# Norm of the second segment among the last output projection, first pair's split weights kept for the second, other PSUM banks

## The chip, the cores and the metric

The kernel runs on one core of a Trainium2 chip. The metric is the device time of one execution in microseconds; the kernel before took 904.81 us, the median of three runs (904.62 to 905.78). The engines are TensorE (PE, with its weight loads as PEld), VectorE (DVE), ScalarE (ACT), GpSimd (POOL) and SyncE (SP), which issues all transfers here. [...]

## The reference

A layer norm with modulation, an attention in four segments with a memory carried from one to the next, and a gated feed-forward part, for 2048 rows of 512 columns, all in fp32. The change lies in the second half. Cut to that:

```python
mod = (_silu(c) @ w_mod).reshape(c.shape[0], 6, 1, -1)
sa, ca, ga, sb, cb, gb = (mod[:, i] for i in range(6))
h = _layernorm(x) * (1 + ca) + sa
x = x + ga * _A_ref(h, A_wq, A_wk, A_wv, A_wo, A_beta)   # attention, its last step is o @ wo
h = _layernorm(x) * (1 + cb) + sb
g = h @ w_gate                       # 512 x 1376
u = h @ w_up                         # 512 x 1376
x = x + gb * ((g * u) @ w_down)      # 1376 x 512
```

## The kernel before, in words

**Precision.** TensorE multiplies in fp32r. An operand is therefore split into a rounded part and the rest, by an ACT copy (hi) and a subtraction on DVE or POOL (lo), and a product is three matmuls: hi x hi, hi x lo, lo x hi (`six`: two such products, six matmuls, for two chunks of the contraction).

**Stages.** Up to about 505 us the attention runs; its steps, the four output projections and the first norm of the feed-forward stage are woven by hand. `wo_op`, `wo_row` and `wo_add` are the output projection of a segment, which ends in x1 = x + projection, written to DRAM (`x1d`). `lnC(s)` (L523) then loads segment s of x1 in four tiles of 128 rows, takes mean and variance on DVE, the root by Ln and Exp on ACT, normalises on DVE (L557), transposes on TensorE (`ctp`, L88), and evicts with the modulation on ACT (`chf`, L566).

**The feed-forward stage** works on pairs of segments: pair 0 is segments 0 and 1, pair 1 is 2 and 3. The 1376 columns of gate and up are eleven tiles of 128, the last (tile 10, `LAST`) of 96. Two neighbouring tiles by the two segments of a pair are one 2 x 2 block product, done with seven products instead of eight. That needs sums of the weights and of the activations:
- `prepare` calls `wprep(n)` (L432) for a unit n, which is gate or up of two tiles: it loads the raw weights `cr`, forms four sums `cs` on POOL (L448 to L452), rounds raw and sums to `cwH` on ACT (L456) and subtracts to `cwL` on POOL (L457). `cwH` and `cwL` are 128 x 1792 fp32, 0.92 MB each, in three slots, slot -n mod 3. For tile 10 `xprep` does the same without sums. `wdprep` (L1244) loads a tile of w_down, multiplies by gb and splits it on DVE and ACT. In pair 0 the down weights of tiles 0, 1 and 10 (`dHp`, `dLp`) lie in the space of weight slot 1.
- `build(p)` (L1171) forms the activations' sums `t` on POOL (L1186) and splits them, `bH` on ACT (L1178), `bL` on DVE (L1179).
- `unit(n)` (L1313) runs the seven products into the banks Z (`sm`), Y (`tb`) and X (`ms0`, `ms1` in turn). ACT copies p1, p5 and y out, DVE adds (c0, c1, c2, L1304), and for up the product g*u (L1299) is formed on POOL or DVE and split into `mH` (ACT, L1240) and `mL` (DVE, L1241). The last two products of a unit (`seven`, `four`, kept in `tail`) are issued in the next unit.
- `direct` (L1361) does tiles 0, 1 and 10 of pair 0 and tile 10 of pair 1 without sums: Xg, Xu of the first segment, with a copy q between the halves, then Yg, Yu of the second. `dirbank` gives its banks in turn from `DB`; before, starting with ms0.
- `down` (L1262) multiplies by the down weights into a bank `acc`, and DVE adds it to `xa` (L1274), which holds x1 and goes to `out` at the end of the pair.

Pair 0 thus starts with lnC(1) and direct tiles 0, 1 and 10 mixed, then down of tiles 0, 1 and 10 for segment 0, then the direct tiles' second segment (the Ys), then units 2, 4, 6, 8. `down` items wait in a list and fill between the products. lnC(2) and lnC(3) run among pair 0's units, build(1) in its last unit.

**What sets the order.** `pe` and `pin` chain TensorE's instructions and the pinned loads by hand in program order. Other instructions are placed by the scheduler, and each engine runs its own in that order. SP issues the transfers in one queue, in order, and with eight completion lanes: each waits for the transfer eight before it. Buffers with a tag and `bufs` are reused in turn, and the next writer waits for the last reader.

## Time and profile before

| | |
|---|---|
| median of three runs | 904.81 us |
| profiled execution | 904.86 us |
| its span (first to last instruction) | 903.1 us |
| TensorE busy, mean granted clock | 856.8 us, 0.990 |
| POOL, DVE, ACT busy | 501.2, 655.1, 475.5 us |
| moved by DMA | 105.70 MB, mean 117 GB/s |
| feed-forward stage, first Xg to last acc | 522.0 to 899.5 us |

A line of the profile gives start, duration, engine, line of the kernel, operation, output <- input, shape, and in brackets the idle time before it and what ended that. In views of stretches the numbers behind the length are busy times of PE, PEld, DVE, ACT and POOL, then TensorE's granted clock, the DMA engines' share and GB/s. Tile names are those of the kernel without buffer numbers. A matmul's duration is longer than the distance to the next, since they overlap; the distance is the pace.

### The profile page before, as it was taken

What the parts mean: (1) busy time and instruction counts of PE and PEld (TensorE: products, weight loads), DVE (VectorE), ACT (ScalarE), POOL (GpSimd) and SP (SyncE); (2) the same over time, 40 slices, a digit from 0 to 9 for tenths busy, and PEclk for the clock granted to TensorE, in tenths of its full rate; (3) what the DMA queues carried; (4) which work ended last, traced back from release to release, by engine and by line L of the source; (5) the groups of instructions that cost most, each with busy time, mean ns of one, the idle gap of its engine ahead of it and who ended that gap; (6) DMA issues with size and microseconds to landing.
All of it is one profiled execution on the core that took longest, in us unless ns stands there. A gap on an engine that the chain in (4) does not pass through costs nothing.

```text
span 903.1 us, 14396 instructions
## 1 busy us (share of the span) xinstructions
PE 856.8 (95%) x4975; PEld 600.8 (67%) x4976; DVE 655.1 (73%) x1711; ACT 475.5 (53%) x725; POOL 501.2 (56%) x607
## 2 busy tenths in 40 slices
PE   8989999989999999999999987989999799999998
PEld 5755656556665566665666665768888577788876
DVE  7598777888788877878886275875956976646544
ACT  3747757687676865767445443433444433343320
POOL 4445536565564763856235326876844977757310
PEclk8999999999999999999999999999999999999999
DMA  7555444554554545466664381213211064211002
GB/s 222 158 159 133 121 111 129 151 158 125 133 133 133 152 145 133 115 185 185 187 209 135 101 282 47 57 37 94 69 50 47 1 197 129 70 47 36 12 1 93
DMA packets 78617, 105.70 MB, mean 117 GB/s; under 512 B 11792, under 2 KB 49680, under 8 KB 78544
## 3 DMA queue, kind: packets, MB, share of 16 engines
q1 hardware_dynamic: 78400, 104.76, 39.4%
q8 instruction: 39, 0.64, 0.3%
q14 instruction: 34, 0.28, 0.1%
q10 hardware_dynamic: 144, 0.02, 0.0%
HBM read 76.43 MB, written 28.05 MB: 116 GB/s over the span
## 4 chain that ended last, share of the span: by engine, by line
PE 71%; DVE 11%; ACT 6%; POOL 6%; DMA 3%; issue 2%; SPq 0%; DVEq 0%; POOLq 0%; ACTq 0%
PE acc L1271 12%; PE tb L85 8%; PE q L85 6%; PE k L85 6%; PE Xg L1216 5%; PE Xu L1216 5%; DVE q L39 5%; PE wops L85 5%; PE vps L85 4%; PE kps L85 4%; PE Yg L1216 3%; PE Yu L1216 3%; PE qps L85 2%; POOL cwL L457 2%; ACT pt L331 2%
## 5 line engine op out<-in xcount | busy, mean ns | idle before, releaser
L39 DVE CUSTOM_DVE_ANT_0 q<-q,cmask 128x384 f32<-128x384 f32 (+3 forms) x512 | 246.6, 508 | 49.9 <-PE q L85 39.8
L331 ACT ACTIVATE pt<-k 128x1024 f32<-128x1024 f32 x160 | 163.8, 1024 | 64.5 <-PE k L85 63.4
L337 POOL TENSOR_SCALAR_AFFINE_SELECT pt<-pt 128x256 f32<-128x256 f32 (+1 forms) x224 | 96.8, 446 | 166.0 <-ACT pt L331 163.7
L85 PE MATMUL q<-kst,qst 96*128 96x384 bf16 (+3 forms) x512 | 101.6, 299 | 11.6 <-DVE nm L39 9.7
L85 PE MATMUL k<-qst,kst 98*128 98x384 bf16 (+3 forms) x512 | 97.1, 302 | 5.0 <-ACT pt L331 4.9
L1274 DVE TENSOR_TENSOR xa<-xa,acc 128x512 f32<-128x512 f32 x95 | 64.7, 682 | 48.0 <-PE acc L1271 46.6
L85 PE MATMUL tb<-pt,v 128*32 128x512 f32 (+3 forms) x1024 | 75.5, 436 | 0.0
L39 DVE DVE_READ_ACCUMULATOR2_ANT nm<- 128x1 f32 x512 | 72.2, 141 | 0.0
L85 PEld LDWEIGHTS <-kst 98*128 98x128 bf16 x512 | 37.7, 98 | 49.5 <-issue 43.3
L85 PEld LDWEIGHTS <-qst 96*128 96x128 bf16 x512 | 43.1, 97 | 38.1 <-issue 14.3
L1271 PE MATMUL acc<-dH,mH 128*128 128x512 f32 (+1 forms) x150 | 59.7, 398 | 2.1 <-ACT mH L1240 2.1
L1271 PE MATMUL acc<-dH,mL 128*128 128x512 f32 (+1 forms) x150 | 59.5, 397 | 0.4 <-DVE mL L1241 0.4
L1271 PE MATMUL acc<-dL,mH 128*128 128x512 f32 (+1 forms) x150 | 59.3, 396 | 0.0
L85 PEld LDWEIGHTS tb<-pt,v 128*32 128x32 f32 x1024 | 28.6, 109 | 38.6 <-issue 33.8
L457 POOL TENSOR_TENSOR cwL<-cr,cwH 128x512 fp32r<-128x512 f32 (+1 forms) x36 | 40.1, 1131 | 21.5 <-ACT cwH L456 21.4
L457 POOL TENSOR_TENSOR cwL<-cs,cwH 128x1024 fp32r<-128x1024 f32 x18 | 48.3, 2684 | 1.2 <-ACT cwH L456 1.2
L1299 POOL TENSOR_TENSOR c0g<-c0g,c0u 128x512 f32<-128x512 f32 x9 | 11.7, 1296 | 56.4 <-DVE c0u L1304 37.7
L363 ACT ACTIVATE tsb<-tb 128x512 f32<-128x512 f32 x32 | 19.0, 595 | 41.0 <-PE tb L85 41.0
L1271 PEld LDWEIGHTS acc<-dH,mH 128*128 128x128 f32 (+1 forms) x150 | 28.2, 188 | 9.9 <-ACT mH L1240 2.5
L1271 PEld LDWEIGHTS acc<-dH,mL 128*128 128x128 f32 (+1 forms) x150 | 28.3, 189 | 7.3 <-DVE mL L1241 0.9
L1271 PEld LDWEIGHTS acc<-dL,mH 128*128 128x128 f32 (+1 forms) x150 | 28.3, 188 | 6.7
L1216 PE MATMUL Xu<-bH,cwH 128*128 128x512 f32 (+1 forms) x68 | 28.1, 413 | 3.5 <-DVE c2u L1304 2.7
(374 smaller groups left out, 2240.3 us busy)
## 6 DMA issues: line engine op xcount, KB each, us to landing
wm<-in_w_mod_dram SPq DMA_DIRECT2D x24, 256.0 KB, 4.0
kd<-k SPq DMA_DIRECT2D x16, 384.0 KB, 2.5
kst<-kd SPq DMA_DIRECT2D x32, 192.0 KB, 3.2
qd<-q SPq DMA_DIRECT2D x16, 384.0 KB, 2.9
qst<-qd SPq DMA_DIRECT2D x32, 192.0 KB, 3.7
crd<-in_w_down_dram SPq DMA_DIRECT2D x20, 256.0 KB, 2.8
cr<-in_w_gate_dram SPq DMA_DIRECT2D x9, 512.0 KB, 3.9
cr<-in_w_up_dram SPq DMA_DIRECT2D x9, 512.0 KB, 4.4
```

What stands on the lines that cost most here:

```text
L39: i = getattr(self.eng, name)(*a, **k)
L85: return pe(nc.tensor.matmul(*a, **k))
L331: ex = act.activation(pt, kp, AF.Exp, scale=0.25)
L337: sels[u, i] = nc.gpsimd.affine_select(w, w, pattern=[[0, w.shape[1]], [1, P]], compare_op=ALU.is_ge, fill=0.0, base=0, channel_multiplier=-1)
L363: act.activation(tsbs[u], tbs.pop(u), AF.Copy)
L457: gp.tensor_sub(wl[:, d], v, wh[:, d].bitcast(F32))
L1216: pe(nc.tensor.matmul(ps[0:n], a, b[:, k], start=first and c == 0, stop=last and c == 5, skip_group_check=True))
L1271: pe(nc.tensor.matmul(ps, a[0:m, t * P:(t + 1) * P], b[0:m], start=j == 0, stop=j == n - 1))
L1274: vec.tensor_add(xa, xa, ps)
L1299: (vec if psum else nc.gpsimd).tensor_mul(g[0:n], g[0:n], v[0:n])
```

## The change

- **lnC(1) earlier.** It is made at slot 2 of the last step, right after the first three groups of `wo_op(3)`: its four loads are issued there, a tile's statistics follow each `wo_row`, Ln and Exp come ahead of the last group of `wo_op(3)`, and the normalisation follows the four `wo_add`. x1_1 lies in the projection's weight pool (`wpool`, tag "orl"), which now stays open to the end. All transposes of segment 1 run between direct tiles 0 and 1, and build(0) starts before direct tile 1.
- **Weights kept.** In pair 0 each unit's cwH and cwL, tile 10's and the down weights' splits are stored to DRAM (`keep`), 59 SP transfers more in all. In pair 1 they are loaded (`fetch`) and each tile is rounded in place by ACT copies of 1024 and 768 columns. POOL's sums and subtractions and DVE's work on w_down disappear there, but for unit 0, which pair 0 never split. Pair 1's units go in the order 2, 4, 6, 8, 0.
- **Other banks.** `ndir` starts at 2, so direct starts with tb and sm, and pair 0's last Ys lie in ms0 and ms1.
- **Less memory.** Temporaries 13 to 8, `add` writes in place, one buffer for cs, one tile for the sums t, so each sum waits until the splits of the one before have been made; the order of the sums is 5, 3, 6, 4, 7. Tile 10 and w_down's last tile are padded with zeros to 128.

```diff
@@ -392,30 +392,56 @@
     LAST = NF - 1
     units = [(0, nm, i) for i in range(2, LAST, 2) for nm in "gu"]
     CH = len(units)
-    units += [(1, "x", LAST)] + [(1, nm, i) for i in range(0, LAST, 2) for nm in "gu"]
+    units += [(1, "x", LAST)] + [(1, nm, i) for i in (2, 4, 6, 8, 0) for nm in "gu"]
     NU = len(units)
+    ENDS = (8, 0)
     wslot, plain = {}, {}
+    wkeep, dkeep = {}, {}
+
+    def keep(key, tiles, store):
+        n = tiles[0].shape[1]
+        store[key] = [dram.tile([P, n], F32, name=f"kept{x}{key[0]}{key[1]}") for x in "HL"]
+        for dst, t in zip(store[key], tiles):
+            nc.sync.dma_start(dst, t.bitcast(F32))
+
+    def fetch(key, tiles, store):
+        for a, d in zip(tiles, store[key]):
+            pin(nc.sync.dma_start(a.bitcast(F32), d))
+        yield
+        n = tiles[0].shape[1]
+        for a in tiles:
+            for i in range(0, n, 1024):
+                b = a[:, i:min(n, i + 1024)]
+                act.activation(b, b.bitcast(F32), AF.Copy)
+                yield
 
     def xprep(n, tag, pool, rpool):
 
-        raw = rpool.tile([P, KT, 2, P], F32, tag="raw0", name=f"cr{n}", bufs=1)
         wh = pool.tile([P, 7, 2, P], F32R, tag=f"wh{tag}", name=f"cwH{n}", bufs=1)
         wl = pool.tile([P, 7, 2, P], F32R, tag=f"wl{tag}", name=f"cwL{n}", bufs=1)
         m = ft[LAST][1]
+        for j, nm in enumerate("gu"):
+            plain[int(n == CH), LAST, nm] = wh[:, 0:4, j], wl[:, 0:4, j]
+        flat = [a.rearrange("p a b c -> p (a b c)")[:, 0:8 * P] for a in (wh, wl)]
+        if n == CH:
+            yield from fetch(("x", LAST), flat, wkeep)
+            return
+        raw = rpool.tile([P, KT, 2, P], F32, tag="raw0", name=f"cr{n}", bufs=1)
+        nc.gpsimd.memset(raw[:, :, :, m:], 0.0)
         for j, w in enumerate((w_gate, w_up)):
             pin(nc.sync.dma_start(raw[:, :, j, 0:m], w.rearrange("(k p) f -> p k f", p=P)[:, :, LAST * P:]))
         yield
-        act.activation(wh[:, 0:4, :, 0:m], raw[:, :, :, 0:m], AF.Copy)
-        nc.gpsimd.tensor_sub(wl[:, 0:4, :, 0:m], raw[:, :, :, 0:m], wh[:, 0:4, :, 0:m].bitcast(F32))
-        for j, nm in enumerate("gu"):
-            plain[int(n == CH), LAST, nm] = wh[:, 0:4, j], wl[:, 0:4, j]
+        act.activation(wh[:, 0:4], raw, AF.Copy)
+        nc.gpsimd.tensor_sub(wl[:, 0:4], raw, wh[:, 0:4].bitcast(F32))
+        yield
+        keep(("x", LAST), flat, wkeep)
         yield
 
...
         for w, nm in ((w_gate, "g"), (w_up, "u")):
-            raws[nm] = raw = rpool.tile([P, KT, P], F32, tag="cr", name=f"cr{nm}{i}", bufs=4)
+            raws[nm] = raw = wpool.tile([P, D], F32, tag="wor", name=f"cr{nm}{i}", bufs=2).rearrange("p (k c) -> p k c", c=P)
             pin(nc.sync.dma_start(raw, w.rearrange("(k p) f -> p k f", p=P)[:, :, i * P:(i + 1) * P]))
         yield 0.0
         gp = nc.gpsimd
@@ -432,15 +458,19 @@
     def wprep(n, tag, pool, rpool):
 
         _, nm, i = units[n]
-        raw = rpool.tile([P, KT, 2, P], F32, tag=f"raw{(n + 1) % 2}", name=f"cr{n}", bufs=1)
+        if (nm, i) not in wkeep:
+            raw = rpool.tile([P, KT, 2, P], F32, tag=f"raw{(n + 1) % 2}", name=f"cr{n}", bufs=1)
         wh = pool.tile([P, 7, 2, P], F32R, tag=f"wh{tag}", name=f"cwH{n}", bufs=1)
         wl = pool.tile([P, 7, 2, P], F32R, tag=f"wl{tag}", name=f"cwL{n}", bufs=1)
         wslot[n] = wh, wl
+        if (nm, i) in wkeep:
+            yield from fetch((nm, i), [a.rearrange("p a b c -> p (a b c)") for a in (wh, wl)], wkeep)
+            return
         views = [w.rearrange("(k p) f -> p k f", p=P)[:, :, i * P:] for w in (w_gate, w_up)]
         gp = nc.gpsimd
         pin(nc.sync.dma_start(raw.rearrange("p k r c -> p k (r c)"), views["gu".index(nm)][:, :, 0:2 * P]))
         yield
-        S = rpool.tile([P, 4, 2, P], F32, tag=f"ws{(n + 1) % 2}", name=f"cs{n}", bufs=1)
...
@@ -1126,6 +1156,8 @@
                 btag[:] = ["ms", "sm", "ms"]
                 us3 = []
                 run(wo_op(3, o3, us3, range(NG - 1), True))
+                lg1 = lnC(1, wpool, lambda: pc, wpool, "orl", 4, lambda name: dbank(name))
+                next(lg1)
             if prev and slot == 4:
                 if (v - 1) % 2 == 0 and v > 8:
                     until((v - 1) // 8, (v - 1) // 2 % 4, 0)
@@ -1150,20 +1182,23 @@
     ps3 = [bank(f"wops3_{t}", shape=(P, 512)) for t in range(4)]
     for t in range(4):
         run(wo_row(ps3[t], t, us3, range(NG - 1)))
+        next(lg1)
     btag[:] = ["sm"]
+    next(lg1)
     run(wo_op(3, o3, us3, (NG - 1,), True))
     for t in range(4):
         run(wo_row(ps3[t], t, us3, (NG - 1,)))
         wo_add(3, t, xr3[t], ps3[t])
+    for t in range(4):
+        next(lg1)
...
-    close(wppool)
...
-    NT, NM = 13, 12
+    NT, NM = 8, 12
...
             pieces[p, j] = hi, lo
 
-        def comb(nm, a, b):
-            r = []
+        T = pc.tile([P, 2, L], F32, tag="ws1", name=f"t{p}", bufs=1)
+
+        def comb(a, b):
             for k in range(2):
-                t = tmp(f"{nm}{p}_{k}")
-                nc.gpsimd.tensor_sub(t, a[k], b[k])
-                r.append(t)
-            return r
-
+                nc.gpsimd.tensor_sub(T[:, k], a[k], b[k])
+            return t
+
+        t = [T[:, k] for k in range(2)]
         b11, b12, b21, b22 = ([hfs[2 * p + c, r][:, k] for k in range(2)] for r in range(2) for c in range(2))
         if p > 0:
             emit(1, b11)
             yield
             emit(2, b21)
             yield
-        t1 = comb("t1", b12, b11)
-        emit(5, t1)
+        emit(5, comb(b12, b11))
         yield
         emit(3, b22)
         yield
-        t2 = comb("t2", b22, t1)
-        emit(6, t2)
-        yield
-        emit(7, comb("t3", b22, b12))
-        yield
-        emit(4, comb("t4", b21, t2))
+        emit(6, comb(b22, t))
+        yield
+        emit(4, comb(b21, t))
+        yield
+        emit(7, comb(b22, b12))
...
@@ -1243,14 +1276,21 @@
 
     def wdprep(p, f, tiles=None):
         f0, n = ft[f]
-        r = tmp(f"crd{p}_{f}")
-        hi, lo = tiles or (bc.tile([P, D], F32R, tag="wd", name=f"d{x}{p}_{f}", bufs=8) for x in "HL")
+        hi, lo = tiles or [bc.tile([P, D], F32R, tag="wd", name=f"d{x}{p}_{f}", bufs=8) for x in "HL"]
+        wds[p, f] = hi, lo
+        if p > 0:
+            yield from fetch(("d", f), (hi, lo), dkeep)
+            return
+        r = tmp(f"crd{p}_{f}") if tiles else wpool.tile([P, D], F32, tag="wor", name=f"crd{p}_{f}", bufs=2)
         pin(nc.sync.dma_start(r[0:n], w_down[f0:f0 + n, :]))
-        yield
-        vec.tensor_mul(r[0:n], r[0:n], gbb[0:n])
-        act.activation(hi[0:n], r[0:n], AF.Copy)
-        vec.tensor_sub(lo[0:n], r[0:n], hi[0:n].bitcast(F32))
-        wds[p, f] = hi, lo
+        if n < P:
+            nc.gpsimd.memset(r[n:], 0.0)
+        yield
+        vec.tensor_mul(r, r, gbb)
+        act.activation(hi, r, AF.Copy)
+        vec.tensor_sub(lo, r, hi.bitcast(F32))
+        yield
+        keep(("d", f), (hi, lo), dkeep)
         yield
 
...
         vec.tensor_add(xa, xa, ps)
-        if fs[0] == LAST - 2:
+        if fs[0] == ENDS[p]:
...
 
-    def add(name, a, b, n=P):
-        r = tmp(name)
-        vec.tensor_add(r[0:n], a[0:n], b[0:n])
-        return r
+    def add(a, b, n=P):
+        vec.tensor_add(b[0:n], a[0:n], b[0:n])
+        return b
 
...
-        finish(p, nm, i, 0, add(f"c0{u}", Z, out_of(f"p1{u}", X)), False)
+        finish(p, nm, i, 0, add(Z, out_of(f"p1{u}", X)), False)
         yield 3
...
         mm(X, 6, False, True)
-        finish(p, nm, i, 1, add(f"c1{u}", X, yy), False)
+        finish(p, nm, i, 1, add(X, yy), False)
...
 
...
     qt = {}
     DB = ["ms0", "ms1", "tb", "sm"]
-    ndir = [0]
+    ndir = [2]
...
     def x_unit(n):
 
-        ndir[0] += 2
         for st in direct(1, LAST, 0):
             yield st
             if st == 1:
@@ -1422,52 +1460,49 @@
             yield from wdprep(p, i + 1)
 
     half = [(c, t) for c in (1, 0) for t in range(4)]
-    lg = lnC(1, pc, pc, pc, "t", NT, dbank)
-    next(lg)
     xp = xprep(-1, 2, pc, pc)
     next(xp)
     dh = pc.tile([P, 7, 2, P], F32R, tag="wh1", name="dHp", bufs=1).rearrange("p a b c -> p (a b c)")
     dl = pc.tile([P, 7, 2, P], F32R, tag="wl1", name="dLp", bufs=1).rearrange("p a b c -> p (a b c)")
     wdp = [wdprep(0, f, (dh[:, j * D:(j + 1) * D], dl[:, j * D:(j + 1) * D])) for j, f in enumerate((0, 1, LAST))]
-    for w in wdp:
+    for w in wdp[:2]:
         next(w)
+    pr0 = prepare(0)
+    next(pr0)
+    next(wdp[2])
     for c, t in half:
         xtile(0, c, t)
     for t in range(4):
         xload2(0, 0, t)
-    pr0 = prepare(0)
-    next(pr0)
     qa = {}
     for f, tag in ((0, "bh7"), (1, "bl7"), (LAST, "bh4")):
         a = pc.tile([P, 2, L], F32, tag=tag, name=f"q0_{f}", bufs=1)
         qa[f] = [a[:, 0], a[:, 1]]
-    for _ in direct(0, 0, 0, qa[0]):
-        next(lg)
+    run(direct(0, 0, 0, qa[0]))
     next(xp)
-    for _ in direct(0, 1, 0, qa[1]):
-        next(lg)
-    next(lg)
+    run(lg1)
+    nb = build(0)
+    next(nb)
+    run(direct(0, 1, 0, qa[1]))
     for w in wdp[:2]:
         next(w)
+    next(nb)
     next(pr0)
-    for _ in direct(0, LAST, 0, qa[LAST]):
-        pass
+    run(direct(0, LAST, 0, qa[LAST]))
     next(wdp[2])
-    next(pr0)
-    nb = build(0)
     for t in range(4):
-        next(lg)
+        next(pr0, None)
         down(0, (0, 1), 0, t)
-    run(lg)
     for t in range(4):
         xload2(0, 1, t)
-    for t in range(4):
-        down(0, (LAST,), 0, t)
-        if t % 2 == 0:
-            next(nb)
     run(pr0)
     pr1 = prepare(1)
     next(pr1)
+    for t in range(4):
+        down(0, (LAST,), 0, t)
+    run(xp)
+    for w in wdp:
+        run(w)
     for f in (LAST, 0, 1):
         for _ in direct(0, f, 1):
             if f != LAST:
...
         for s in (2, 3):
-            yield from lnC(s, pc, (bc, pc)[s % 2], pc, "t", NT, dbank)
+            yield from lnC(s, wpool, lambda: (bc, pc)[s % 2], wpool, "orl", 4, dbank)
...
         pr = prepare(n + 2)
+        if p == 0:
+            keep((nm, i), [a.rearrange("p a b c -> p (a b c)") for a in wslot[n]], wkeep)
         if n == CH - 1:
             nb = build(1)
         for st in (unit if nm != "x" else x_unit)(n):
...
+    close(wppool)
     close(B["bcpool"])
...
```

More of the change, by code (lines that the diff above doesn't have):

```diff
@@ L442, in wprep @@
         yield
-        S = rpool.tile([P, 4, 2, P], F32, tag=f"ws{(n + 1) % 2}", name=f"cs{n}", bufs=1)
+        S = rpool.tile([P, 4, 2, P], F32, tag="ws0", name=f"cs{n}", bufs=1)
         def A(r, c):
@@ L561, in lnC @@
             if d % 2 == 0:
-                hfs[s, d // 2] = hpool.tile([P, 2, L], F32, tag=f"hf{s % 2}{d // 2}", name=f"chf{s}_{d // 2}", bufs=1)
+                hfs[s, d // 2] = hpool().tile([P, 2, L], F32, tag=f"hf{s % 2}{d // 2}", name=f"chf{s}_{d // 2}", bufs=1)
             ps = bk(f"ctp{s}_{d}")
@@ L568, in lnC @@
                 if d % 2 == 0:
-                    pieces[0, 1 + d // 2] = tuple(hpool.tile([P, 2, L], F32R, tag=f"b{x}{1 + d // 2}", name=f"b{x}0_{1 + d // 2}", bufs=1)
+                    pieces[0, 1 + d // 2] = tuple(hpool().tile([P, 2, L], F32R, tag=f"b{x}{1 + d // 2}", name=f"b{x}0_{1 + d // 2}", bufs=1)
                                                   for x in "hl")
@@ L1013, in fill_b @@
         small = lambda name: bank(name, small=True)
-        lg = lnC(0, pb, bc, pb, "x1", 4, small)
+        lg = lnC(0, pb, lambda: bc, pb, "x1", 4, small)
         pr = prep(0, bc, pb)
@@ L1350, in seven @@
             mm(X, 7, False, True)
-            finish(p, nm, i + 1, 1, add(f"c2{u}", X, p5), False)
+            finish(p, nm, i + 1, 1, add(X, p5), False)
         def four():
@@ L1385, in direct @@
             mm(Y, nm, 1, 3, False, True)
-            finish(p, nm, f, 1, add(f"c1{nm}{p}_{f}", Y, q, n), False)
+            finish(p, nm, f, 1, add(Y, q, n), False)
             yield 4
```

## The prediction

> **What bounds the kernel now.** I read the page first, then the busy time of each engine in stretches of 20 us over the feed-forward stage, then TensorE's waits there, then the chain of waits, and last the timeline at the places that the change touches.
>
> ```profile
> span 903.1 us, 14396 instructions
> PE 856.8 (95%) x4975; PEld 600.8 (67%) x4976; DVE 655.1 (73%) x1711; ACT 475.5 (53%) x725; POOL 501.2 (56%) x607
> ```
>
> TensorE is busy 95% of the span, so a gain can only come from its idle time. The changed lines act from about 505 us on. In the next view the columns are the stretch, its length, the busy time of each engine, TensorE's granted clock, and the DMA share and GB/s.
>
> ```profile
> 520.00:540.00 20.00, 18.06 (x77) 13.43 (x76) 15.10 (x28) 9.37 (x19) 4.08 (x4) 1.00 0.96 317
> 540.00:560.00 20.00, 14.89 (x61) 10.57 (x60) 14.06 (x18) 7.28 (x11) 16.80 (x13) 0.91 0.15 54
> 600.00:620.00 20.00, 17.25 (x68) 13.11 (x67) 14.56 (x18) 8.98 (x18) 19.36 (x19) 0.91 0.20 63
> 700.00:720.00 20.00, 15.22 (x58) 10.48 (x57) 18.03 (x18) 9.48 (x17) 20.00 (x14) 0.93 0.00 0
> 720.00:740.00 20.00, 20.00 (x86) 15.41 (x85) 17.42 (x19) 6.66 (x11) 16.06 (x13) 0.99 0.54 172
> ```
>
> TensorE is short of 20 us in a few places only. At 520 to 540 the DMA engines are full. At 700 to 720 POOL is busy for all of it. Its waits between 520 and 900 (what waited, for whom: us in total, times, longest):
>
> ```profile
> PE acc L1271 <- DVE xa L1274: 3.7, 3, 3.0
> PE Xu L1216 <- DVE c2u L1304: 2.7, 2, 2.3
> PE Zg L1216 <- POOL cwL L457: 2.3, 1, 2.3
> PE Zg L1216 <- DVE c1u L1304: 2.1, 1, 2.1
> PE acc L1271 <- ACT mH L1240: 2.1, 1, 2.1
> PE ctp L88 <- DVE x L557: 1.3, 2, 0.8
> PE Xg L1216 <- DVE c1g L1304: 1.3, 1, 1.3
> PE Xg L1216 <- ACT q L1374: 0.9, 1, 0.9
> ...
> PE Xg L1216 <- POOL cwL-1_6784 L409: 0.8, 1, 0.8
> ...
> PE acc L1271 <- DVE mL L1241: 0.4, 1, 0.4
> PE Xu L1216 <- ACT q L1374: 0.3, 1, 0.3
> ```
>
> The chain of waits gives the places (start, us, what):
>
> ```profile
> 522.00 1.41 PE Xg L1216 x6
> ...
> 525.55 5.63 DMA cr-1_6782<-in_w_up_dram
> ...
> 559.50 2.79 PE Yg L1216 x12
> ...
> 578.39 1.66 PE Zg L1216 x6
> ...
> 607.35 2.00 PE Zg L1216 x5
> ...
> 719.42 1.99 PE Xu L1216 x6
> ...
> 772.32 1.66 PE Xg L1216 x6
> ...
> 876.76 22.69 PE acc L1271 x96
> ```
>
> The last row is the undisturbed pace: 22.69 / 96 = 0.236 us a matmul, 1.40 for six. A six that restarts after an idle time takes 1.66, 0.27 more; the one at 719.42 takes 1.99, because the clock was halved. The timeline shows the half clock as matmuls 0.43 apart instead of 0.23:
>
> ```profile
> 553.15 0.65 PE L1271 MATMUL acc<-dHp,mH 128*128 128x512 f32 x1 [2.95 <-DVE xa L1274]
> ...
> 554.02 0.63 PE L1271 MATMUL acc<-dLp,mH 128*128 128x512 f32 x1
> 554.45 0.63 PE L1271 MATMUL acc<-dHp,mH 128*128 128x512 f32 x1
> ```
>
> The three stretches below clock 1.00 hold one such period each: 0.09 x 20 = 1.8, 1.8 and 0.07 x 20 = 1.4 us, about 1.7 us each. From 522.00 to the end of the last row (899.45) are 377.5 us. The program's own work there is 1476 matmuls of 512 columns and 48 transposes, counted in the compiled order of both kernels, which have the same TensorE instructions; at the pace it is 348. So idle time, refills and half clock come to about 29 us, the bound of any gain: 904.86 - 29 = 876.
>
> **The change part by part.** All sums are against the profiled execution: 904.86 us, 1.76 outside the span, 0.05 above the median 904.81.
>
> *Stage A: the second norm moved, up to the first Yg of tile 10 (559.50 before).* The stage holds 108 matmuls and 16 transposes (0.11 each): 27 of its 37.5 us. Its loss of 10.6 is the waits 3.7 + 1.3 + 0.9 + 0.8 + 0.3 = 7.0, a half-clock period of 1.7, and seven refills of 0.27. The move takes four loads of x1 and their statistics from behind 522 into the last output projection. On SP those loads stood ahead of the x weights:
>
> ```profile
> 523.17 1.86 SPq L528 DMA_DIRECT2D x<-x1d  x4
> 525.07 0.43 SPq L406 DMA_DIRECT2D cr-1_6782<-in_w_gate_dram  x1
> ```
>
> So the x weights (cr-1) are issued 1.9 us earlier, the last of them at 523.6. They took 5.6; without the megabyte ahead of them, 3.3 us at 317 GB/s, it would be 2.3. I take 3.6, landed at 527.2, and 529.2 at worst. The wait for xa, which stood behind the builds' bL on DVE, and that for the normalised x fall away: the builds move ahead, and x is normalised in the tail of the projection, where TensorE has matmuls of its own. In its place the transposes now stand between the two direct tiles. ACT's and DVE's orders there are set by three durations:
>
> ```profile
> 543.45 0.78 ACT L566 ACTIVATE chf<-ctp,modc 128x512 f32<-128x512 f32 x1 [3.01 <-PE ctp L88]
> ```
> ```profile
> 567.54 4.41 DVE L1179 TENSOR_TENSOR bL<-t,bH 128x512 fp32r<-128x512 f32 x1 [1.76 <-ACT bH L1178]
> ...
> 572.48 0.68 DVE L1179 TENSOR_TENSOR bL<-t,bH 128x512 fp32r<-128x512 f32 x1
> ```
>
> I walked ACT's new order by hand, with 0.6 for each other copy of 512 columns (the 1024-wide one, quoted below, takes 1.05). The fourth transpose reuses the bank of an earlier one and waits for that one's chf, which stands behind the x weights' copy: 527.2 + 1.05 + 0.78 + 0.6 + 0.78 = 530.4. TensorE is there after direct(0,0) and twelve transposes, at 528.7: 1.7 idle. The second half of direct(0,1) waits for its copy q, behind two more chf, two dHp, two cwH (0.9) and two bH: 530.4 + 1.56 + 1.2 + 0.9 + 1.2 + 0.6 = 535.9, some waits between them put it at 536.8, TensorE comes at 534.0: 2.8 idle. The second half of tile 10 waits for a q behind mH0_1_0, and so behind DVE's gs0_1_0. DVE has eleven two-input SBUF operations queued from 528 on, while POOL has twelve of its own. The rows above show what that does: a bL of 0.68 took 4.41 while POOL ran without a gap. Taking one DVE operation for each POOL operation, 11 x (0.68 + 1.0) puts gs at 546.5 and q at 548; TensorE, 24 matmuls after 536.8, comes at 542.5: 5.5 idle. Together 10.0, three refills 0.8, and one half-clock period 1.7, since the last idle is longer than the 2.95 that brought one on: 12.5 against 10.6. I take **A at -1.9**. Without the DVE and POOL conflict the third idle is 1.0 and the half clock goes: 6.3, so +4.3. With the x weights at 529.2 and a second half-clock period: -5.
>
> [...]
>
> *Stage B: banks.* Zg0_2 followed Yu0_1 in the same bank and waited 2.1 for DVE to empty it. With the direct tiles starting two banks on it follows nothing that is late, and its weights were split by 571: **+2.4** (2.1 and a refill); bounds 0 and 2.4.
>
> *Stage C: the wait for cwL at 607 (2.3 and a half clock).* The slot still comes free with the last product of tiles 0 and 1, and POOL still makes this split in the first pair. **+0.3**; bounds -1.7 (a longer wait) and +2.0 (clock spared).
>
> *Stage D: 610 to 690.* Each split is now also stored: 2 x 0.92 MB a unit, a unit being (607.35 - 578.39 - 2.75) / 2 = 13.1 us, 140 GB/s beside the 63 of the stretch from 600. The full stretch above carried 317, so TensorE, which waited for nothing here, covers it: 0; if a store holds up a load behind it on SP, the cover I find by hand is 5 us. Bounds 0 and -2, which take in the smaller pools as well: eight temporaries for thirteen, sums in place and one buffer for cs, at none of which the order walked here stops an engine that TensorE awaits.
>
> *Stage E: 690 to 722.* Here POOL is the bound:
>
> ```profile
> 707.64 1.19 POOL L448 TENSOR_TENSOR cs<-cr 128x256 f32<-128x256 f32 x1
> 708.80 1.23 POOL L451 TENSOR_TENSOR cs<-cr 128x256 f32<-128x256 f32 x1
> ...
> 713.44 1.20 POOL L449 TENSOR_TENSOR cs<-cs,cr 128x256 f32<-128x256 f32 x1
> 714.61 1.75 POOL L1299 TENSOR_TENSOR c2g<-c2g,c2u 128x512 f32<-128x512 f32 x1
> ```
>
> The three cs ahead of c2g belong to a split that is now fetched: 3.6 us less ahead of c2g, mH and mL, which TensorE awaited for 2.1 and 0.4, and DVE's c2u (2.3) is no longer held by this queue. The loss here is 4.8 idle, 1.7 half clock and 0.8 in refills, 7.3. My walk leaves mH and mL of tile 9 ready 0.7 to 1.3 us before use; I leave 1.0 for that thin cover. **+6.3**; bounds +2 (mH late by 3.6 and the half clock kept) and +7.3.
>
> *Stage F: the rest of pair 1.* The idles of 0.4 (c2u) and 1.3 (c1g) behind POOL's late sums go with 0.5 of refills, 2.2. What a fetched unit costs and saves:
>
> ```profile
> L457 POOL TENSOR_TENSOR cwL<-cs,cwH 128x1024 fp32r<-128x1024 f32 x18 | 48.3, 2684 | 1.2 <-ACT cwH L456 1.2
> L456 ACT ACTIVATE cwH<-cs 128x1024 fp32r<-128x1024 f32 x18 | 18.9, 1049 | 2.8 <-POOL cs L452 2.8
> ```
>
> ACT copies 2 x 1792 elements at that rate, 3.7 us instead of 2.1, and POOL loses the 2.7 shown, four cs of 1.2 and two narrower subtractions. In ACT's order the copies stand ahead of evictions that release TensorE's banks. At 317 GB/s the two halves land in 5.8 us, and I find 2.8 us of slack at the tightest unit, and up to 1.5 us of wait at the first. **+1.5**; bounds -3 (half a us of wait on six units) and +2.2.
>
> The sum: -1.9 + 2.4 + 0.3 + 0 + 6.3 + 1.5 = 8.6, so 904.86 - 8.6 = 896.3: **896**.
>
> **The rivals.** (1) *The early norm works out fully*: DVE and POOL do not collide in A, A is +4.3 instead of -1.9, and E and F give their bounds, 1.7 more: 888.4. For it: q of direct tiles waited only 0.9 before. Against it: the 4.41 row. (2) *Copies crowd ACT*: its copies come behind evictions that TensorE awaits, and E and F give 3 instead of 7.8: 901. For it: mH is already awaited for 2.1; against: ACT is busy 6.7 to 9.5 of 20 us there. (3) *Slower: the fetch is slow.* A fetch lands late, ACT stands at its copy, and the evictions behind it hold TensorE's banks. It decides below 214 GB/s, where 1.84 MB takes 8.6, the 5.8 and the slack of 2.8. At the 172 GB/s of 720 to 740 it takes 10.7 us, 2.1 over the slack, on seven units 14.5: 911. For it: nothing shown of pair 1 moved more than that. Against: it is what was asked for, not a limit, since the share of the DMA engines is 0.54 there. (4) *The POOL work removed was hidden anyway*: TensorE is idle in pair 1 only near 700 to 720 and at 772; if the builds' longer order (each sum waits for DVE's last bL) takes that back, E and F are 0: 904.1.
>
> **How the numbers follow.** Forecast 0.52, rival 1 0.13, rival 2 0.13, rival 3 0.15, rival 4 0.07. The likeliest is 896, with 892 to 901 of its own (A's bounds against each other). The range of 887 to 905 takes in rivals 1, 2 and 4 and leaves out rival 3 and the ends. Of these, about 1.8 us (0.2%, what a measurement of this kernel can tell from no change) part the classes at 903.0 and 906.6: faster 0.52 + 0.13 + 0.13 less 0.02 for an A worse than its bound, 0.76; same 0.07; slower 0.15 + 0.02 = 0.17.
>
> **What would show it.** A: first Yg of tile 10 at about 560, idles of 1.7, 2.8 and 5.5 at the fourth transpose, direct(0,1) and tile 10, bL of several us on DVE. B: no idle ahead of Zg0_2. C: the wait for cwL at the second Zg still about 2. E: POOL below 20 in the stretch before the second pair and clock 1.00 there. F: no ACT copy that waits for its DMA longer than 2 us. It is wrong if A costs over 5, if waits for ACT (p5, y, mH) appear at each unit of pair 1, or if a fetch takes over 8 us from issue to landing.

## The result, and the profile after

| | before | after |
|---|---|---|
| median | 905.03 us (904.62 to 905.78) | 899.26 us (898.74 to 899.54) |
| profiled execution, span | 904.86, 903.1 us | 899.35, 897.6 us |

The changed kernel takes 0.9935 of the time of the kernel before, interval 0.9917 to 0.9952: 5.8 us less, where 8.6 were forecast. The page of the changed kernel:

```profile
span 897.6 us, 14464 instructions
PE 855.1 (95%) x4976; PEld 600.3 (67%) x4976; DVE 623.5 (69%) x1689; ACT 496.3 (55%) x745; POOL 426.8 (48%) x552
```

POOL has 74 us less work, DVE 32 less and ACT 21 more. That the end moved by 5.5 only is read from TensorE's stretches. The columns are those of the prediction:

```profile
520.00:540.00 20.00, 15.98 (x71) 12.62 (x70) 14.98 (x17) 12.32 (x21) 12.46 (x9) 0.91 0.92 313
540.00:560.00 20.00, 17.12 (x66) 12.00 (x65) 13.09 (x16) 4.92 (x8) 12.14 (x9) 0.91 0.50 176
560.00:580.00 20.00, 19.98 (x87) 15.40 (x85) 13.81 (x14) 6.09 (x10) 12.53 (x10) 1.00 0.51 171
580.00:600.00 20.00, 18.25 (x73) 14.53 (x72) 13.69 (x22) 6.29 (x14) 6.67 (x8) 0.91 0.39 132
600.00:620.00 20.00, 17.22 (x70) 13.50 (x69) 14.70 (x19) 9.41 (x16) 17.58 (x18) 0.91 0.55 203
620.00:640.00 20.00, 20.00 (x94) 16.29 (x93) 11.79 (x19) 8.04 (x12) 15.26 (x14) 1.00 0.92 322
...
700.00:720.00 20.00, 19.97 (x87) 14.97 (x86) 16.01 (x23) 16.67 (x27) 8.78 (x6) 1.00 0.58 214
720.00:740.00 20.00, 17.88 (x71) 13.71 (x70) 5.79 (x9) 6.29 (x9) 1.29 (x1) 0.91 0.62 211
```

From 700 to 720 POOL went from 20.0 to 8.8 and TensorE has no hole there any more. But there are five stretches with a half-clock period now, where there were three. TensorE's five longest groups of waits from 505 on, as in the prediction's view:

```profile
PE Xg L1249 <- ACT q L1413: 5.4, 2, 2.7
PE Yg L1249 <- ACT p5g L1363: 3.9, 2, 2.1
PE Zg L1249 <- POOL cwL L487: 2.3, 1, 2.3
PE ctp L88 <- ACT chf L596: 1.3, 1, 1.3
PE Xu L1249 <- DVE yu L1343: 0.9, 1, 0.9
```

The waits of over 0.1 us for c2u, mH and xa have gone, and of the two for c1u the longer one (2.1). The other, 0.8 us at 872 in the kernel before, is still there as the 0.9 for yu, since the sum is now written in place. In their place TensorE waits for ACT: for q in stage A, and twice for p5g, a kind of wait that the kernel before did not have.

The stages, measured in each profile between the same four points on TensorE (starts of matmuls on the timeline; the end is that of the last acc):

| stage | before | after | gain | forecast |
|---|---|---|---|---|
| A: first Xg (521.84, 520.45) to first Yg of tile 10 (559.34, 558.32) | 37.5 | 37.9 | -0.4 | -1.9 |
| B: to Zg of tiles 4 and 5 (604.58, 604.38) | 45.2 | 46.1 | -0.8 | +2.4 |
| C, D, E: to the first Zg unit of pair 1 (731.0, 724.4) | 126.4 | 120.0 | +6.4 | +6.6 |
| F: to the end of the last acc (899.44, 893.78) | 168.5 | 169.4 | -0.9 | +1.5 |
| sum | 377.6 | 373.3 | +4.3 | +8.6 |

The other 1.4 us of the 5.7 lie ahead of all that: the first Xg starts 1.4 us earlier. That comes from the first 25 us, which the change does not touch. TensorE had waited 1.88 us up to 17.37 before and 1.75 up to 17.39 after; two stretches of before, then the same of after:

```profile
15.00:20.00 5.00, 3.12 (x18) 2.89 (x17) 4.56 (x11) 1.45 (x2) 0.00 (x0) 0.75 0.45 165
20.00:25.00 5.00, 5.00 (x17) 4.09 (x16) 3.89 (x7) 3.55 (x5) 0.00 (x0) 0.57 0.36 107
```
```profile
15.00:20.00 5.00, 3.25 (x26) 2.88 (x25) 4.58 (x11) 1.45 (x2) 0.00 (x0) 1.00 0.47 170
20.00:25.00 5.00, 4.07 (x14) 2.03 (x13) 4.07 (x7) 4.78 (x8) 0.00 (x0) 1.00 0.36 107
```

One execution fell into a half-clock period (0.75, 0.57) and the other did not. In the fourteen profiles of this study the first Xg starts between 519.8 and 522.4, with either attention code (the kernel before with the banks alone: 519.9). It is chance, so the stages are compared from the first Xg on, and a median is read with 1 to 2 us of doubt.

### The profile page after: what moved, and what is told of

The parts are those of the page before. It is cut to its first block, busy times and chain, and to the rows that moved or that the text cites. A ratio compares the mean times of both kernels' runs of the same rounds, so it can differ in the third digit from the quotient of the medians.

```text
span 897.6 us, 14464 instructions
## 1 busy us (share of the span) xinstructions
PE 855.1 (95%) x4976; PEld 600.3 (67%) x4976; DVE 623.5 (69%) x1689; ACT 496.3 (55%) x745; POOL 426.8 (48%) x552
## 4 chain that ended last, share of the span: by engine, by line
PE 72%; DVE 14%; ACT 6%; POOL 3%; DMA 2%; issue 2%; SPq 0%; POOLq 0%; ACTq 0%; DVEq 0%
PE acc L1311 12%; PE tb L85 7%; PE q L85 6%; PE k L85 6%; PE Xg L1249 6%; PE Xu L1249 6%; DVE q L39 5%; PE wops L85 4%; PE vps L85 4%; PE Yu L1249 3%; PE kps L85 3%; PE Yg L1249 3%; PE qps L85 3%; ACT pt L331 2%; PE Zu L1249 1%
## 5 line engine op out<-in xcount | busy, mean ns | idle before, releaser
L331 ACT ACTIVATE pt<-k 128x1024 f32<-128x1024 f32 x160 | 163.8, 1024 | 64.4 <-PE k L85 63.7
L85 PEld LDWEIGHTS <-qst 96*128 96x128 bf16 x512 | 43.1, 97 | 37.9 <-issue 14.0
L1339 POOL TENSOR_TENSOR p1g<-p1g,p1u 128x512 f32<-128x512 f32 x9 | 11.7, 1295 | 95.1 <-DVE p1u L1343 95.1
L85 PE MATMUL kps<-ahH,wkH 128*128 128x512 f32 x64 | 29.7, 464 | 0.6 <-DVE ahH L39 0.6
L85 PE MATMUL wops<-woH,oH 128*128 128x512 f32 x64 | 28.3, 442 | 0.7 <-ACT oH L512 0.7
L85 PE MATMUL qps<-ahH,wqH 128*128 128x512 f32 x64 | 28.7, 448 | 0.0
```

Of the source, the lines that this page charges most:

```text
L85: return pe(nc.tensor.matmul(*a, **k))
L331: ex = act.activation(pt, kp, AF.Exp, scale=0.25)
L1339: (vec if psum else nc.gpsimd).tensor_mul(g[0:n], g[0:n], v[0:n])
```

## The experiments

The stages of all runs, in us, as in the table above (C to E in one), and the median with its ratio to the kernel before on the same chip. The stages are those of one profile each.

| run | A | B | C-E | F | median, ratio (interval) |
|---|---|---|---|---|---|
| before | 37.5 | 45.2 | 126.4 | 168.5 | |
| changed | 37.9 | 46.1 | 120.0 | 169.4 | 899.3, 0.9935 (0.9917-0.9952) |
| e1 banks alone | 40.1 | 45.6 | 126.9 | 167.7 | 905.4, 0.9998 (0.9983-1.0013) |
| e2 old banks | 37.9 | 47.5 | 121.0 | 167.2 | 899.5, 0.9928 (0.9905-0.9952) |
| e3 nothing kept | 37.8 | 48.4 | 126.0 | 167.7 | 905.1, 0.9988 (0.9970-1.0007) |
| e4 norm late | 40.3 | 46.8 | 120.8 | 169.5 | 900.8, 0.9947 (0.9928-0.9965) |
| e5 copies late | 37.8 | 46.1 | 120.1 | 165.4 | 896.8, 0.9909 (0.9881-0.9937) |
| e6 product on DVE | 37.8 | 46.8 | 120.8 | 167.4 | 899.8, 0.9934 (0.9913-0.9956) |
| e7 sums on DVE | 38.4 | 44.2 | 120.3 | 168.2 | 898.6, 0.9928 (0.9900-0.9955) |
| e8 filler | 37.8 | 46.0 | 121.3 | 167.6 | 897.7, 0.9915 (0.9893-0.9936) |
| e9 p5g first | 37.9 | 43.0 | 120.3 | 167.3 | 895.2, 0.9888 (0.9861-0.9914) |
| e10 q first | 33.3 | 44.5 | 120.3 | 168.4 | 891.6, 0.9852 (0.9831-0.9873) |
| e11 e5 + e9 + e10 | 35.8 | 43.0 | 120.2 | 165.4 | 890.3, 0.9831 (0.9805-0.9856) |
| e12 e11 and filler | 32.0 | 43.1 | 120.6 | 165.5 | 887.8, 0.9801 (0.9778-0.9824) |

**e1, the banks alone.** The kernel before, with this (a bank is one of the eight tiles of 128 x 512 fp32 that the kernel keeps in PSUM and its matmuls write):

```diff
-    ndir = [0]
+    ndir = [2]
-        ndir[0] += 2
```

> The kernel before with the bank order of the change alone. Theory (the bank change is worth its 2.1 us wait and a refill, and what ate it in the changed kernel is ACT's order, where the copy p5g stands behind mH of tile 1): here the compiled order has p5g ahead of that mH, so Zg0_2 and the second Yg both start without a wait of over 0.5 us, and the time is 2.4 us under the kernel before, about 902.6. Rival (the copy's wait always takes the place of the bank wait): 904.5 to 905.5, with an idle time of over 1.5 us ahead of the second Yg.

The time did not change (0.9998). The wait ahead of Zg0_2 (the first Zg of tiles 2 and 3) has gone, and three others came, which the kernel before had not: two of them on the timeline, the third (1.5 us for cwL, ahead of a Yg at 612.9, in stage C) in the waits.

```profile
582.76 0.50 PE L1216 MATMUL Yg<-bH,cwH 128*128 128x512 f32 x1 [0.99 <-ACT p5g L1324]
588.45 0.50 PE L1216 MATMUL Zu<-bh,cwH 128*128 128x512 f32 x1 [1.25 <-DVE c0g L1304]
```

So the rival holds, though in pieces (the wait for p5g is 0.99, not over 1.5): ACT and DVE are a little behind TensorE after the Ys, and the bank was only where that showed first. A is 40.1 here, 2.6 more than in the other profile of this attention code, with a wait of 1.4 for q in place of 0.3 and a second half-clock window (552.1 to 559.0). Whether the banks or chance did that is open, so the 37.5 of the kernel before is itself good to some 2 us only.

**e2, the old banks in the changed kernel.** The reverse edit.

> The changed kernel with the bank order of before. Theory (in the changed kernel the bank change lost as much as it won: 2.1 us and a refill won, then 1.75 us of wait for p5g, a refill and a half-clock period of 1.7 lost): 898 to 899, with the wait of about 2 us ahead of Zg0_2 back and no half clock at 580 to 600. Rival, the prediction's stage B (+2.4): 901.7.

The median is nearer to the theory, and cannot be told from that of the changed kernel (899.3), but the account is another: the wait for Zg0_2 is 3.5 us here and brings a half-clock period of its own, B is 1.4 longer, and F is 2.1 shorter because the wait for p5g in the second pair happens to be 1.5 there, without a half clock.

**e3, nothing kept.** Without `keep` and `fetch` in all three preparations; the second pair's weights are made from the raw ones, in the new order of units.

> The changed kernel without the stores and fetches: the second pair's weights are split anew from the raw ones, as before. Theory (POOL's load was the bound at 690 to 722, and the fetch gave back 4.1 of the 9.5 us lost in the second pair): POOL full again near 700 to 720, waits for mH, c2u and the clock below 1.00 there, 904 to 905. Rival (that POOL work was hidden, and the order of the second pair's units makes the gain): 899 to 900.

This is the theory's case: 905.1, and C-E back to 126.0. POOL is busy for 18.4 of 20 us, TensorE waits 2.7 us there, and the clock falls:

```profile
700.00:720.00 20.00, 16.68 (x64) 11.98 (x62) 16.86 (x18) 10.94 (x20) 18.40 (x14) 0.91 0.00 0
```

Storing and fetching wins 6.0 us in C-E and loses 1.7 in F. B is 2.4 longer here as well, with a wait of 3.4 for p5g and two half-clock windows; why is not shown. Without storing and fetching the rest of the change gives nothing that can be measured (0.9970 to 1.0007).

**e4, the norm late.** The loads, statistics and normalisation of segment 1 put back behind the projection, and the block from `xp = xprep` to the Ys in the order of before.

> The changed kernel with the second norm back behind the projection (loads, statistics and normalisation where they were) and its transposes again among the products of the down weights. Theory (the early norm won 7 us of waits and lost 7 us of others and a second half-clock period): no difference beyond 1.5 us, 898 to 900.5. Rival, the prediction's stage A (-1.9): 897.4. A gain by the early norm that the stage's ends do not show: over 901.

The median, 900.8, is at the edge of what was expected; the profiled execution took 905.4, the upper end of its runs. In it A is 40.3, 2.4 longer, with half clock from 533.6 to 540.4 and from 557.5 to 564.3: with x1's loads on SP in front of them, the tiles of w_down land at 531.8, DVE's product with gb and ACT's dHp follow, and q of tile 1 stands behind dHp on ACT, 5.2 us of wait. Within this kernel the early norm is worth some 1.5 (medians, whose intervals overlap) to 2.4 us (one profile each). Against the kernel before (37.5) it is worth nothing that shows. There w_down lands no earlier (532.0), but ACT has q of tile 1 at 528.9, ahead of dHp; in e4 it comes at 535.3, behind two dHp. The order on ACT makes that wait. The stores, which the kernel before does not have, do not: e4 issues its first at 531.9, when w_down has landed.

**e5, the fetched copies late.**

```diff
             pin(nc.sync.dma_start(a.bitcast(F32), d))
         yield
+        yield
...
-                act.activation(b, b.bitcast(F32), AF.Copy)
+                pin(act.activation(b, b.bitcast(F32), AF.Copy))
```

> The changed kernel with the ACT copies of a fetched weight one step later and held behind the TensorE work issued before them, so that p5g of the second pair's first unit stands ahead of the copy of cwL that waits 6.9 us for its transfer. Theory (TensorE's wait of 2.1 us for p5g at 732 is ACT standing at a copy whose transfer has not landed; a refill and a half-clock period follow from it): that wait under 0.3 us, clock 1.00 from 720 to 740, 4 us less from the first Zg of the second pair to the last acc (165.4 instead of 169.4). Rival (the bank or the product itself is late): the wait stays over 1.5 us, or comes back at the next evictions.

F is 165.4, as the theory said to a tenth. (The interval of the whole time overlaps that of the changed kernel; the 4.0 us are read from the stage.) ACT in the changed kernel, then in this one:

```profile
729.96 1.79 ACT L415 ACTIVATE cwL<-cwL 128x1024 fp32r<-128x1024 f32 x2 [4.01 <-DMA cwL<-keptLg]
731.65 0.58 ACT L1363 ACTIVATE p5g<-Yg 128x512 f32<-128x512 f32 x1
```
```profile
728.23 0.60 ACT L1364 ACTIVATE p5g<-Yg 128x512 f32<-128x512 f32 x1 [2.86 <-PE Yg L1250]
728.72 1.05 ACT L416 ACTIVATE cwL<-cwL 128x1024 fp32r<-128x1024 f32 x1
```

The copy had stood 4.0 us at a transfer (6.86 us long, issued at 723.02 when the slot came free), with p5g behind it. The weight was needed only at 753.

**e6, the last product on DVE.**

```diff
-        (vec if psum else nc.gpsimd).tensor_mul(g[0:n], g[0:n], v[0:n])
+        (vec if psum or (p, f, c) == (0, 1, 1) else nc.gpsimd).tensor_mul(g[0:n], g[0:n], v[0:n])
```

> The changed kernel with the last product g*u of tile 1, second segment, on DVE instead of POOL. Theory (p5g of the first unit stands behind mH of that product on ACT, and the product took 1.67 us on POOL against 0.68 on DVE): mH and p5g come about 1 us earlier, the wait of 1.75 us ahead of the second Yg falls to 0.5 to 1.0, the half clock at 583 goes, 2.5 to 3 us less from the first Yg to Zg0_4 (46.1 before the edit). Rival (dH, which stands between them and waits for DVE, sets it): wait unchanged within 0.3 us.

The rival: the wait is 1.91. DVE's product took 1.19 beside POOL and delayed crd, and with it dH, which stands right ahead of p5g on ACT.

**e7, the sums on DVE.** In `comb`, `vec` instead of `nc.gpsimd` for the first pair.

> The changed kernel with the first pair's activation sums t on DVE instead of POOL. Theory (in stage A DVE's two-input operations alternate with POOL's, each holding the other up, and this makes the 2.7 us wait for q of tile 10): POOL has eight operations less, DVE's bL and crd come down to 0.7 to 1.2 us, the wait falls by 1 us or more and its half clock may go: stage A 35 to 37 instead of 37.9 us. Rival (DVE's own queue is the limit, and eight more operations of 0.68 lengthen it): the wait grows to over 3.5 us.

Neither in A: the two waits for q are 3.4 and 2.2 instead of 2.7 and 2.7, A 38.4. From 540 on bL takes 0.68, but DVE has the eight sums to make as well (0.68 each, 2.76 for one of them beside POOL): the two cancel. B is 1.9 shorter, since the wait for p5g fell to 1.25 and brought no half clock.

**e8, filler.** Ahead of both waits for q, six matmuls into a bank that nobody reads. The first of the two places:

```diff
+        if i == 1:
+            six(dbank("dum0"), *plain[0, 0, "g"], lambda k: (k,), P, *pieces[0, 1], True, True)
```

> The changed kernel with six matmuls of no use (their bank is not read) ahead of the two waits for q in stage A. They take 1.4 us of each 2.7 us wait and do not delay what follows. Theory (a 3.41 us window in which TensorE idles for about half of it is followed by one at half clock): both half-clock periods of the stage go, matmuls 0.23 apart after each wait, stage A 34.5 us instead of 37.9. Rival (the half clock follows from the wait's end, whatever the idle time): half clock stays, 37.9.

After the first wait the clock is whole; the changed kernel first, then this one, each with the matmul that waited and two later ones:

```profile
534.81 0.50 PE L1249 MATMUL Xg<-bh,gH 128*128 128x512 f32 x1 [2.73 <-ACT q L1413]
...
536.25 0.63 PE L1249 MATMUL Xg<-bh,gL 128*128 128x512 f32 x1
536.68 0.63 PE L1249 MATMUL Xg<-bl,gH 128*128 128x512 f32 x1
```
```profile
534.26 0.50 PE L1249 MATMUL Xg<-bh,gH 128*128 128x512 f32 x1 [1.39 <-ACT q L1413]
...
535.29 0.39 PE L1249 MATMUL Xg<-bh,gL 128*128 128x512 f32 x1
535.52 0.39 PE L1249 MATMUL Xg<-bl,gH 128*128 128x512 f32 x1
```

But A did not move. The matmul that waits for q of tile 10 still started 24.5 us after the first Xg, and what TensorE had saved it waited there: 3.0 us even behind its filler, and a half clock after it. So with this order the chain of DVE and ACT is what limits A, not the clock.

**e9, p5g first.** mH of tile 1's second segment and dH of tile 3 are held behind p5g and p1g of the first unit. The core of it, cut (dH of tile 3 is held by lines of the same kind):

```diff
-        split(p, f, c, g)
+        if (p, f, c) in ((0, 1, 1),):
+            late.append(lambda: split(p, f, c, g, pin))
+        else:
+            split(p, f, c, g)
...
+            if n == 0 and st == 6:
+                while late:
+                    late.pop()()
```

> The changed kernel with two ACT operations put behind p5g and p1g of the first unit: mH of tile 1, second segment, and dH of tile 3, none of which is needed before the unit's end. Theory (ACT's order alone makes the wait of 1.75 us ahead of the second Yg, with a refill and a half-clock period): wait under 0.3 us there, clock 1.00 from 580 to 600, 46.1 us from the first Yg to Zg0_4 become 42.4. Rival (another wait takes its place, as in the run with the banks alone): over 44.5, with waits for c0, cwL or acc that were not there.

B is 43.0, 3.1 less; a new wait of 0.3 for yg and its refill make most of the rest. ACT's rows, in order, in the changed kernel, where mH and dH stand ahead of p5g, then in this one:

```profile
580.42 0.63 ACT L1273 ACTIVATE mH<-q 128x512 fp32r<-128x512 f32 x1 [1.74 <-POOL q L1339]
580.96 0.61 ACT L1290 ACTIVATE dH<-crd 128x512 fp32r<-128x512 f32 x1
581.48 0.58 ACT L1363 ACTIVATE p5g<-Yg 128x512 f32<-128x512 f32 x1
```
```profile
578.37 0.60 ACT L1372 ACTIVATE p5g<-Yg 128x512 f32<-128x512 f32 x1
580.06 0.60 ACT L1372 ACTIVATE p1g<-Xg 128x512 f32<-128x512 f32 x1 [1.09 <-PE Xg L1249]
580.55 0.62 ACT L1275 ACTIVATE mH<-q 128x512 fp32r<-128x512 f32 x1
```

**e10, q of tile 10 first.** In the same manner mH of tile 1's first segment, bH of product 6 and the first unit's cwH come behind q.

> The changed kernel with four kinds of ACT operations (mH of tile 1 first segment, the sums' bH of product 6, the first unit's cwH) put behind the copies q of tile 10 that they stood ahead of. Theory (ACT stands behind DVE's and POOL's backlog, and q itself is ready at once): the wait of 2.7 us ahead of tile 10's second half falls under 0.6 and its half clock goes; the backlog shows at the down products instead, for mL or dLp, with 1 to 2 us: stage A 35 to 36.5 instead of 37.9. Rival (the backlog itself is the limit and what is won comes back in full): 37.4 to 38.5.

More than expected: A is 33.3, the wait for q of tile 10 is gone, and the backlog does not show at the down products. ACT has q at 541.22, right when TensorE has finished, where it had 544.29. Of the 7.7 us in the medians the edit accounts for A's 4.5; in the profile B and F are 1.6 and 1.0 shorter by luck, since the two waits for p5g (1.8 and 1.7) brought no half clock there. The half clock that is left came after the wait for tile 1's q:

```profile
PE Yg L1249 <- ACT p5g L1368: 3.5, 2, 1.8
PE Xg L1249 <- ACT q L1418: 2.6, 1, 2.6
PE Zg L1249 <- POOL cwL L487: 2.3, 1, 2.3
```

**e11, all three edits of order.**

> The changed kernel with the three edits of order together: fetched copies late, p5g first, q of tile 10 first. If they add: 4 us in the second pair, 3.7 ahead of Zg0_4 and 2 in stage A, about 889.5 against 899.3 for the changed kernel in the same state. If the stage A edit only moves its wait: 891.5. If the p5g edit is taken by other waits as well: 895.

They add, but for A: there the wait for tile 1's q is 3.95 (dHp again behind w_down's landing), with two half-clock windows after it. That this is chance is not shown; for it speaks that in e12, with the same edits, filler and wait together take 2.8, near the wait of 2.6 in e10.

**e12, e11 and filler.** Nine matmuls ahead of that wait (cut):

```diff
+            for j in range(9):
+                pe(nc.tensor.matmul(dum, wh[:, j % 2], bh[:, j % 2], start=j == 0, stop=j == 8))
```

> The kernel with all three edits of order, and nine matmuls of no use (their bank is not read) ahead of the wait for q of tile 1, 2.1 us of a wait that was 2.6 to 3.9 us. Nothing behind that wait stands in for it any more, so if the half clock comes from idle time within a 3.41 us window, both half-clock periods there (5.1 us of matmuls 0.43 apart, 2.5 us lost) go, and stage A is 33.3 to 34 us instead of 35.8, the time 888 to 889. Rival (half clock after the wait all the same, or the filler delays the real matmuls): 35.8 or more, 890 to 892.

A is 32.0 and the median 887.8: 17.6 us under the kernel before and some 11 to 12 under the changed one. No half clock is left in A, and nothing behind the filler gives the time back: A is 1.3 under e10, which has no filler, and 3.8 under e11. What the filler alone is worth in the whole time is not settled, since the intervals of e11 and e12 overlap. The filler and the wait:

```profile
532.42 2.20 PE L1501 MATMUL dum<-bh,gH 128*128 128x512 f32 x9
535.27 0.50 PE L1250 MATMUL Xg<-bh,gH 128*128 128x512 f32 x1 [0.64 <-ACT q L1423]
535.61 0.40 PE L1250 MATMUL Xg<-bh,gL 128*128 128x512 f32 x1
```

## Why the prediction was right, and where it was not

**Right: where the gain lies.** Stage E was forecast at +6.3 and C to E gave +6.4 against 6.6; e3 shows that it is the kept weights (126.0 without, 120.0 with). The cover of 1.0 us left for mH and mL of tile 9 was not used up. Rival 4 (that POOL work was hidden anyway) falls by e3. Rival 3 (a slow fetch) came true at one unit: its two halves landed 10.2 us after the first was issued (723.02 to 733.25), and TensorE waited 2.1. That this is the price which the rival set is luck; the second half was issued 3.2 us after the first. At two more units the halves took 8.2 and 8.7, over the 8 us that were named as a sign of being wrong, and TensorE did not wait. ACT stood 4.0 us at the late copy, twice the 2 us named as a sign for F.

**Right in kind, wrong in size: A (-1.9, measured -0.4, with the doubt named at e1).** The three waits came at the three places named, 1.3, 2.7 and 2.7 us instead of 1.7, 2.8 and 5.5. The step that was mis-sized is "Taking one DVE operation for each POOL operation, 11 x (0.68 + 1.0)": gs came at 542.1 instead of 546.5, as POOL was not always there to alternate with (it stood idle from 539.33 to 539.96, and the bL that began at 539.80 took 0.68). Nor does the 4.41 row show one for one: three POOL operations end while that bL lasts.

```profile
540.41 1.77 DVE L1214 TENSOR_TENSOR bL<-t,bH 128x512 fp32r<-128x512 f32 x1
542.10 0.67 DVE L1339 TENSOR_TENSOR gs<-gs,Xu 128x512 f32<-128x512 f32 x1
```

On the other side there were two half-clock periods, not one. Rival 1 (the conflict does not show) falls with these rows: bL took up to 1.8 us, though not the several us that were expected. The forecast's own range, 892 to 901, does not come out of A's bounds either: 896.3 less 6.2 or plus 3.1 is 890.1 to 899.4.

**Wrong: B (+2.4, measured -0.8).** The failing step is "it follows nothing that is late". It looked at the bank that Zg0_2 goes to and not at what stands in ACT's order next: the second Yg needs its bank emptied by p5g, and ACT had mH of the last Y and dH ahead of it. The wait of 2.1 became 1.75, and the half clock that the 2.1 before had escaped (1.0 of it fell into one clock window and 1.15 into the next) came with it. Shown by e9 (3.1 us back by order alone), and by e1, where the banks alone give nothing.

**Wrong: F (+1.5, measured -0.9).** The mis-sized step is "up to 1.5 us of wait at the first" unit: the wait came there, but it was 2.1, and the sum left out the refill and the half clock that follow it. e5 measures all three: 4.0 us. Without them F gains 3.0, more than the upper bound of 2.2. Rival 2 (copies crowd ACT) was thus half true: it is not ACT's load, but its order at one unit.

**C and D (+0.3 and 0, within C to E).** The wait for cwL stayed at 2.3 with its half clock, as forecast. In D one wait of 0.3 us for mL at 650 is all that shows; 322 GB/s from 620 to 640 were carried without another.

The sum was off by 4.3 us in the stages, 3.2 of it in B and 2.4 in F, less 1.5 in A; chance at the start gave 1.4 back.

## What to carry to other kernels

Follow the engine that empties a bank, not only the bank: when a wait is removed, look at what is queued ahead of the next eviction on that engine, above all copies that wait for a transfer (4.0 us ahead of p5g in F) or for another engine (mH, 1.74 for POOL, ahead of p5g in B), and put the evictions first. A short stall on TensorE cost more than its length here when it took over half of a clock window of 3.41 us: 1.75 us at 582 in the changed kernel, and 1.7 more at half clock. Where the operands are late anyway, matmuls that nobody reads can fill the gap (A is 32.0 in e12 and 33.3 in e10), but that helped only where nothing behind the gap waited for the same late engine (in e8 A is 37.8, in the changed kernel 37.9).

## What the runs showed of the hardware

**The clock falls after about half a window of idle time.** In these profiles the half-clock stretches begin and end on a grid of 3.41 us whose phase differs from one execution to the next. From 505 us to the last acc the trace of the kernel before has the granted clock at 0.50 from 553.34 to 556.76, 607.96 to 611.37 and 717.18 to 720.60, that of the changed kernel from 535.33 to 538.75, 545.57 to 548.99, 583.12 to 586.53, 607.01 to 610.43 and 733.31 to 736.72. Each lasts 3.41 us, and from start to start it is 16 and 32 times that in the first, 3, 11, 7 and 37 times in the second. Three windows in turn of the changed kernel, with TensorE's busy time ahead of the other engines' and its clock third from the end:

```profile
579.71:583.12 3.41, 1.66 (x7) 1.05 (x6) 2.16 (x3) 2.12 (x4) 3.33 (x5) 1.00 0.20 76
583.13:586.52 3.39, 3.39 (x9) 2.65 (x8) 3.27 (x5) 0.60 (x1) 0.92 (x1) 0.50 0.61 155
586.54:589.94 3.40, 3.40 (x16) 2.79 (x15) 2.01 (x3) 0.00 (x0) 0.00 (x0) 1.00 1.05 389
```

In nine profiles (before, changed, e1, e3 to e6, e8, e11) the half-clock stretches fix the grid to 0.5 us. Summing TensorE's idle time over its windows there, each window with 1.75 us or more before the last acc (some thirty of them, up to 3.0) is followed by one at half clock, and none with 1.67 us (e6) or less is: about half of a window. The border is not sharp: in e7, which is not among the nine, the granted clock gives a grid by which the window from 603.4 holds 1.8 us, and the clock stays whole after it. The same wait for p5g shows it on both sides, in the changed kernel and in e10:

```profile
582.11 0.50 PE L1249 MATMUL Yg<-bH,cwH 128*128 128x512 f32 x1 [1.75 <-ACT p5g L1363]
...
583.15 0.63 PE L1249 MATMUL Yg<-bH,cwL 128*128 128x512 f32 x1
```
```profile
577.99 0.50 PE L1249 MATMUL Yg<-bH,cwH 128*128 128x512 f32 x1 [1.77 <-ACT p5g L1368]
...
579.03 0.39 PE L1249 MATMUL Yg<-bH,cwL 128*128 128x512 f32 x1
```

In the first the whole 1.75 fell into one window. In the second the half clock from 535.48 on (matmuls 0.43 apart from 535.53) sets a window's start at 576.44, twelve windows later, so 0.2 of the 1.77 fell into the window before. Once the clock is halved, less is enough: 0.7 to 1.1 us in such a window (e1, e8, e11, e3) kept it so for another, and 0.4 did not (before, e9). In e4 it stayed halved from 557.5 to 564.3 over matmuls without idle time, twelve of them with 96 rows; why is open. This is also why the same stall costs 1.7 us, half of a window, more in one execution than in the next.

**DVE and POOL hold each other up** when both work on SBUF. From 505 us on, DVE's operations of 128x512 with two inputs in SBUF (bL, mL, dL, dLp, crd) took 0.68 to 0.70 us wherever POOL did nothing beside them, in all 28 of the kernel before and all 35 of the changed one. Beside POOL they took 0.67 to 4.41 (76, the median 1.15) and 0.67 to 2.29 (51, the median 1.18). POOL's products and sums of 128x512 took 1.29 to 1.30 with DVE idle (11 and 10) and in the median 1.72 and 1.66 beside such an operation (25 and 21). DVE's sums from a PSUM bank (xa) kept to 0.65 to 0.69 beside POOL too (56 and 30). In stage A of e10 the same bL took 0.68 to 1.78 (1.78 where a sum on POOL lasted from 538.70 to 540.37). Often they alternate, one operation each: from 530.17 to 539.88 of the changed kernel seven operations of DVE end 0.55 us behind one of POOL each. The 4.41 us of the kernel before, with three POOL operations, shows that they need not.
